# Rotary attention with a channel mix on one core: both parts of a pair's product with V in one stretch

## Chip, cores and metric

The kernel runs on one core of a Trainium2 chip (trn2). The metric is the device time of one execution in microseconds (us), as the median of several runs. Everything below is read from one execution that the hardware profiler recorded.

## What is computed

For 8 batches, 8 heads, 576 positions and a head size of 64, q and k get a rotary embedding, softmax attention is computed, and its output x (8 x 576 x 512) goes through a channel mix with 1024 hidden channels:

```
q_rot, k_rot = rotate(q), rotate(k)
scores = (q_rot @ k_rot.T) / 8
attn = exp(scores - max) / (sum + 1e-9)
x = attn @ v                                  # heads side by side: B, S, 512
xk = mu_k * x + (1 - mu_k) * x_prev           # x_prev: x one position earlier
xr = mu_r * x + (1 - mu_r) * x_prev
out = sigmoid(xr @ w_r) * (relu(xk @ w_k) ** 2 @ w_v)
```

## The kernel before

**Pairs and units.** Two heads make a pair, and there are 32 pairs, 4 to a batch. A pair's 576 query positions are cut into five units (`plan_unit`, L422): units 0 to 3 hold 128 positions of both heads and use the array in two row halves of 64, and unit 4 holds the last 64 positions of both heads in one full-height product. A unit's scores are written by TensorE (L439), reduced to the negated maximum by VectorE (L450), and exponentiated by ScalarE with the row sums as a by-product (L460).

**Plain and split.** Score products come in two kinds. In a plain pair the operands are taken as fp32 (one product per half of the keys, which the trace shows as two instructions). In a split pair q and k are cut into a rounded high part and a remainder, and three products of the faster type fp32r are added up. Splitting takes, for q and for k, one copy (L280 or L282, the high part) and one subtraction (L276, the low part) more than a plain pair needs. `PLAIN` = 5 makes pairs 0 to 4 plain.

**Turning the probabilities.** The product with V needs the keys on the partitions. Pairs 0 to 3 (`EARLY`) are turned by TensorE (L485). From pair 4 on, VectorE transposes blocks of 32 x 32 (L465), one DMA writes the result to DRAM (`turned`, L528) and another reads it back (`rows`, L532). This goes in two parts per pair: part 0 is units 0 and 1 (256 columns for TensorE), part 1 is units 2 to 4 (320 columns). There is one buffer of `rows` for each part, and one buffer for the pair's V (`values`).

**The product with V** (`plan_values`, L542) is, for each part, one item of the plan: 20 matrix products (L557) into one PSUM tile. VectorE then multiplies by the inverse row sums (L564, L569), which have come over DRAM (`sums` to `inv` to `rb`, L507, L513). The channel mix of a batch reads x only after both parts of the pairs concerned (`d["X", half]` holds the results of both).

**The channel mix** (`plan_channel_mix`, L696) makes the mixed operands (L608 to L613), splits them, and runs products of full array height and width, three per step (L637, L638, L639).

**What sets the order.** Nothing is ordered by hand. `Plan.op` takes each item with an engine, a rank, a modelled cost, its predecessors and its buffers. `Plan.issue` (L113 to L210) plays the whole program through a small model: whenever an engine is free, it takes the ready item of least rank, and the order found there is the order in which every engine's instructions, and SP's DMA issues, stand in the program. The ranks come from the constants `R`, `EARLY_R`, `PB`, `MB` and the biases `B_...`. For TensorE an item has a class (0 full array, 1 row halves, 2 the product with V in column halves); a change of class costs `SWITCH` in the model, and `STICK` lightly favours the class at hand. On the chip, the array is used in those three shapes.

Of the kernel before, what the change touches and what calls it, by code (L numbers as in the profile page):

```python
# [23 lines left out]

P = 128
PT = 18
PLAIN = 5
GROUPS = ((0, 1), (2, 3, 4))
WG = (128, 160)
EARLY = 4  # L30
R = dict(k=593.56, q=-116.24, v=661.21, cs=925.67, mu=674.34, ld=2714.96, rope0=616.81, rope1=2781.36, rope2=-26.1,
         split0=3595.69, split1=-1160.76, u0=-579.99, u1=-488.68, u2=-113.46, u3=-1056.0, u4=-253.44, mx=-366.15,
         ex=-1682.84, tp=733.33, di=882.16, dm=-14.89, da=-1213.51, dw=-1363.97, dr2=1693.46, av=2178.52,
         ah=176.61, nr=-1468.99, ev=-1092.53, m0=94.65, mh=99.21, mk=-452.8, mr=761.94, ms=243.4, mx1=50.11,
         mx2=-219.51, mx3=-849.63, mg=17.74, mv=10.72, dr=-638.56, key0=-1530.69, key1=1921.97, key2=337.31,
         gate0=1607.52, gate1=71.52, wk0=458.16, wk1=557.26, wr0=-1023.28, wr1=-291.81, wv0=-546.55, wv1=82.66)
EARLY_R = dict(k=-702.46, q=-1811.61, v=-1186.3, ld=-2648.41, rope0=1279.56, rope1=1357.91, rope2=-489.45,
               split0=-2142.88, split1=2554.98, u0=579.81, u1=-2897.73, u2=-1335.35, u3=-546.57, u4=-1160.48,
               mx=1309.7, ex=308.02, tp=-2491.01, di=1519.96, dm=-694.43, da=-742.07, dw=-1706.94, dr2=1268.99,
               av=-49.56, ah=1124.92, nr=848.06, ev=-2067.99)  # L40
PB = (-3437.67, -442.86, -1619.42, -811.31, 1408.72, -35.97, -277.17, 549.82)
B_COPY, B_ROPE, B_SPLIT, B_LOW, B_MIX, B_SQUARE, B_RELU = -1693.57, -394.58, 857.22, 1457.27, 1935.83, -1161.27, -1219.61
MB = (-201.34, -365.74, -405.66, -1336.49, 1020.79, -1176.32, -311.37, 202.48)
CY = 12
SWITCH, STICK = 195, 20.0
BUFS = dict(nat=2, kh=2, kl=1, qh=2, ql=1, vs=1, pe=4, pe3=8, p0=1, p1=1, s=2, s3=3, nm=6, sums=2, rb=1, pt0=1, pt1=1, t=2, xT=5, raw=2, mxf=2, mxh=5, mxl=5, acc=2, hr=2, kkh=8, kkl=8, rt=3)


# [8 lines left out]
def dve(n):  # L57
    return 1.04 * n + 70
# [16 lines left out]
class Plan:  # L75
# [37 lines left out]
    def issue(self):  # L113
        ops = self.ops
        wait = [len(o[4]) + len(o[6]) for o in ops]
        then = [[] for _ in ops]
        for i, o in enumerate(ops):
            for x in o[4]:
                then[x].append(i)
        left = {s: s.users for f in self.families.values() for s in f}  # L120
        follows = {}
        for f, slots in self.families.items():
            slots.sort(key=lambda s: (s.group, ops[s.opener][1], s.index))
            for n, s in enumerate(slots):
                s.index, s.wait = n, int(n >= self.bufs[f]) + int(n > 0 and slots[n - 1].opener != s.opener)
                if n > 0 and slots[n - 1].opener != s.opener:
                    follows.setdefault(slots[n - 1].opener, []).append(s)
        behind = [[] for _ in ops]
        for i, o in enumerate(ops):
            for x in {s.opener for s in o[5]} - {i}:  # L130
                behind[x].append(i)
                wait[i] += 1
        ready = {e: [] for e in self.LATENCY}
        busy = {e: False for e in self.LATENCY}
        port = {"V": 0.0, "G": 0.0}
        events = []
        now, engine, last = 0.0, {}, 0

        def met(i):
            wait[i] -= 1  # L140
            if wait[i] == 0:
                for e in ops[i][0]:
                    heapq.heappush(ready[e], (now if e == "D" else ops[i][1] + ops[i][0][e][1], i))

        def grant(s, producer=None):
            s.wait -= 1
            if s.wait <= 0:
                if producer is None:
                    met(s.opener)
                else:  # L150
                    later(producer, s.opener)

        def later(producer, o):
            heapq.heappush(events, (now + self.LATENCY[producer][next(iter(ops[o][0]))], 1, o))

        def finish(i, e):
            for x in then[i]:
                later(e, x)
            for s in ops[i][5]:
                left[s] -= 1  # L160
                if left[s] == 0:
                    slots = self.families[s.family]
                    if s.index + self.bufs[s.family] < len(slots):
                        grant(slots[s.index + self.bufs[s.family]], e)

        for i, w in enumerate(wait):
            if w == 0:
                wait[i] = 1
                met(i)
        for slots in self.families.values():  # L170
            for s in slots:
                if s.wait == 0:
                    met(s.opener)
        while True:
            for e, queue in ready.items():
                while queue and not busy[e]:
                    if e == "T":
                        best = min(queue, key=lambda x: (x[0] + STICK * (self.cls[x[1]] != last), x[1]))
                        queue.remove(best)
                        i = best[1]  # L180
                    else:
                        _, i = heapq.heappop(queue)
                    if i in engine:
                        continue
                    engine[i] = e
                    ops[i][3](e)
                    for s in follows.get(i, ()):
                        grant(s)
                    for x in behind[i]:
                        met(x)  # L190
                    busy[e] = True
                    cost, _, shared = ops[i][0][e]
                    if e == "T":
                        cost += SWITCH * (self.cls[i] != last)
                        last = self.cls[i]
                    start = now
                    if shared:
                        start = max(now, port["G" if e == "V" else "V"])
                        port[e] = start + cost
                    heapq.heappush(events, (start + cost, 0, i))  # L200
            if not events:
                break
            now, kind, i = heapq.heappop(events)
            if kind == 1:
                met(i)
                continue
            busy[engine[i]] = False
            finish(i, engine[i])
        assert len(engine) == len(ops), [(i, ops[i][0], ops[i][1], wait[i]) for i in range(len(ops)) if i not in engine][:20]
        return now  # L210
# [3 lines left out]
def rope_attention_channel_mix(ctx, tc, qt, kt, v, cs, mu, w_k, w_v, w_r, out):  # L214
# [4 lines left out]
    B, NP, _, _, S = kt.shape  # L219
# [202 lines left out]
    def plan_unit(t, d, c):  # L422

        heads = (0, 1) if c < 4 else (0,)
        w = {}
# [12 lines left out]
                        r = (up, dn)[x] if c < 4 else whole  # L438
                        T.matmul(w[x][:, h, 0:H], lhsT=kind(d[q][r, c * P:(c + 1) * P]), rhs=kind(d[k][r, h * H:(h + 1) * H]), start=i == 0, stop=i == len(todo) - 1)  # L439

        m = op("T", t, (1100 if d["plain"] else 770) if c < 4 else (1072 if d["plain"] else 804), products, d["q"] + d["k"] + ([] if d["early"] else early_done), slots + d["sq"] + d["sk"], int(c < 4))
        for x in heads:
            u = 4 if c == 4 else c + 5 * x
            g = int(c >= 2)
# [49 lines left out]
    def plan_move(t, d):  # L494
# [18 lines left out]
            nc.sync.dma_start(d["rb"][(up, dn)[x]], src)  # L513

        c4 = op("A", t + d["r"]["ex"] + 0.2, 170, lambda: A.copy(d["sums"][:, 9:10], d["sums"][:, 4:5]), [d["E", 4]], [ss])
        o = op("V", t + d["r"]["nr"], 400, inverse, [c4] + [d["E", u] for u in range(9)], [ss])
        o = dma(t + d["r"]["dw"], P * 128, write, [o], [ss])
        d["R"] = [dma(t + d["r"]["dr2"] + 0.1 * x, D * 4 * 640, lambda x=x: read(x), [o], [sr]) for x in range(2)]
        d["sr"] = sr
# [22 lines left out]
    def plan_values(t, d):  # L542


        w, e = {}, [[], []]
        sx = d["sx"] = Slot("xT")
        for g in range(2):
            s_a = Slot("t")
# [17 lines left out]
            def divided_last(x):  # L566
                r = (up, dn)[x]
                acc = w[1][:, 0:384].rearrange("p (a n) -> p a n", a=4)[r, :, 80 - 80 * x:96 - 80 * x]
                V.tensor_tensor(out=d["x"][r, 513:S + 1].rearrange("p (a n) -> p a n", n=16), in0=acc, in1=d["rb"][r, :, 128 + 16 * x:144 + 16 * x], op=ALU.mult)  # L569

            o = op("T", t + d["r"]["av"] + d["r"]["ah"] * g, 2120 + 490 * g, products, d["M", g] + [d["v"]], [s_a, d["sv"], d["spt", g]], 2)
            e[g] = [op("V", t + d["r"]["ev"] + d["r"]["ah"] * g, dve(256) + 30, divided, [o] + d["R"], [s_a, sx, d["sr"]])]
            if g:
                e[g] += [op("V", t + d["r"]["ev"] + d["r"]["ah"] * g + 0.1 * x, dve(64) + 30, lambda x=x: divided_last(x), [o] + d["R"], [s_a, sx, d["sr"]]) for x in range(2)]
        z = op("G", t + d["r"]["ev"], 110, lambda: G.memset(d["x"][:, 0:1], 0.0), [], [sx])
        d["X", 0], d["X", 1] = e[0] + e[1] + [z], e[0] + e[1]

# [220 lines left out]
```

## Time and profile before

| | |
|---|---|
| median of 3 runs | 974.1 us (970.01 to 974.42) |
| profiled execution | 972.62 us, span in the trace 970.8 us |
| TensorE busy (matrix products) | 905.7 us, 93% |
| VectorE busy | 793.9 us, 82% |
| ScalarE busy | 574.0 us, 59% |
| GpSimd busy | 501.1 us, 52% |
| DMA | 248.23 MB, 256 GB/s on average |
| mean granted TensorE clock | 0.985 of full speed |

TensorE's matrix products overlap in the trace: one is shown with about 0.3 us, and the next starts 0.13 us later. What one costs is read from start to start, not from its length.

### The profile page before, as it was taken

The numbers are of one execution on the slowest core, as the hardware profiler recorded it, in microseconds if no ns is written. First come the engines' busy times: TensorE is split into PE (matmuls) and PEld (weight loads), VectorE is DVE, ScalarE is ACT, GpSimd is POOL, SyncE is SP. The second block draws the span as 40 slices with busy tenths as digits, with TensorE's granted clock in tenths as the row PEclk, the third lists the DMA queues.
The fourth block names the chain that finished last, engine by engine and source line by source line (L and its number), as shares of the span: only waits on it lengthen the run. The fifth ranks groups of instructions, "written<-read, shape, count | busy, mean of one in ns | idle before, by whom it ended". The sixth has DMA issues, their size and how long they took to land.

```text
span 970.8 us, 18627 instructions
## 1 busy us (share of the span) xinstructions
PE 905.7 (93%) x6938; PEld 758.1 (78%) x6938; DVE 793.9 (82%) x1348; ACT 574.0 (59%) x1414; POOL 501.1 (52%) x491
## 2 busy tenths in 40 slices
PE   0767879999899999999999999989999999999998
PEld 0444558888688788888988888777898888888998
DVE  5787898898788988989897879978986988974652
ACT  4776767675566665755665647647665656734243
POOL 6766764563566646666265636356654734601201
PEclk9898999999899999999999999999999999999999
DMA  7553538979999979986978688798976788793000
GB/s 251 159 172 120 163 99 301 381 277 340 338 321 336 331 267 347 332 303 232 324 270 290 198 314 305 260 371 313 374 256 234 275 306 271 255 373 95 20 26 25
DMA packets 98107, 248.23 MB, mean 256 GB/s; under 512 B 11360, under 2 KB 43104, under 8 KB 90848
## 3 DMA queue, kind: packets, MB, share of 16 engines
q1 hardware_dynamic: 98016, 247.04, 72.0%
q8 instruction: 54, 0.88, 0.4%
q14 instruction: 37, 0.30, 0.1%
HBM read 154.47 MB, written 92.54 MB: 254 GB/s over the span
## 4 chain that ended last, share of the span: by engine, by line
PE 73%; DMA 13%; DVE 6%; ACT 3%; POOL 2%; issue 2%; SPq 1%; DVEq 0%; ACTq 0%; POOLq 0%
PE acc L637 17%; PE acc L638 14%; PE acc L639 14%; PE av L557 14%; PE scores L439 12%; DMA rb<-inv 4%; DMA rows<-turned 2%; DMA values<-in_v 2%; DVE nm L450 2%; DMA inv<-sums 2%; PE turn L485 1%; DMA xk<-in_kt 1%; DVE p L465 1%; ACT early L460 1%; DMA turns<-in_cs 1%
## 5 line engine op out<-in xcount | busy, mean ns | idle before, releaser
L460 ACT ACTIVATE pe<-scores,nm 128x576 f32<-128x576 f32 x252 | 184.7, 737 | 127.0 <-DVE nm L450 126.4
L450 DVE TENSOR_REDUCE nm<-scores 128x1 f32<-128x576 f32 x288 | 206.0, 747 | 43.8 <-PE scores L439 42.3
L465 DVE STREAM_TRANSPOSE p<-pe 128x576 f32<-128x576 f32 x252 | 186.1, 760 | 5.9 <-ACT pe L460 5.3
L557 PE MATMUL av<-rows,values 128*64 128x320 f32 (+1 forms) x1280 | 170.6, 414 | 6.3 <-DMA rows<-turned 2.4
L637 PE MATMUL acc<-mxh,wk_h 128*128 128x288 f32 x512 | 158.8, 310 | 3.4 <-DVE mxh L282 2.4
L637 PE MATMUL acc<-kkh,wv_h 128*128 128x288 f32 x512 | 155.4, 303 | 0.7 <-DVE rt L693 0.6
L276 POOL TENSOR_TENSOR mxl<-mxf,mxh 128x288 fp32r<-128x288 f32 x90 | 79.0, 883 | 145.7 <-ACT mxh L280 102.7
L638 PE MATMUL acc<-mxl,wk_h 128*128 128x288 f32 x512 | 151.0, 295 | 1.1 <-POOL mxl L276 1.1
L638 PE MATMUL acc<-kkl,wv_h 128*128 128x288 f32 x512 | 151.1, 295 | 0.0
L639 PE MATMUL acc<-kkh,wv_l 128*128 128x288 f32 x512 | 151.0, 295 | 0.0
L639 PE MATMUL acc<-mxh,wk_l 128*128 128x288 f32 x512 | 150.6, 294 | 0.0
L557 PEld LDWEIGHTS av<-rows,values 128*64 128x64 f32 x1280 | 88.7, 138 | 68.0 <-issue 14.6
L439 PE MATMUL scores<-kh,qh 64*128 64x288 f32 (+1 forms) x666 | 112.5, 390 | 25.5 <-POOL qh L276 20.2
L276 POOL TENSOR_TENSOR kkl<-hr,kkh 128x288 fp32r<-128x288 f32 x95 | 82.0, 873 | 82.5 <-ACT kkh L280 68.5
L276 POOL TENSOR_TENSOR xq<-xq,turns 128x128 f32<-128x128 f32 (+1 forms) x79 | 82.7, 1062 | 62.5 <-DMA xq<-in_qt 62.5
L439 PEld LDWEIGHTS scores<-kh,qh 64*128 64x128 f32 (+1 forms) x666 | 64.3, 197 | 63.8 <-issue 25.2
L637 PEld LDWEIGHTS acc<-mxh,wk_h 128*128 128x128 f32 x512 | 96.4, 188 | 18.5 <-issue 10.1
L637 PEld LDWEIGHTS acc<-kkh,wv_h 128*128 128x128 f32 x512 | 96.2, 188 | 10.6 <-issue 7.5
L638 PEld LDWEIGHTS acc<-mxl,wk_h 128*128 128x128 f32 x512 | 96.6, 189 | 1.6 <-POOL mxl L276 1.5
L639 PEld LDWEIGHTS acc<-mxh,wk_l 128*128 128x128 f32 x512 | 96.4, 188 | 0.0
L638 PEld LDWEIGHTS acc<-kkl,wv_h 128*128 128x128 f32 x512 | 96.3, 188 | 0.0
L639 PEld LDWEIGHTS acc<-kkh,wv_l 128*128 128x128 f32 x512 | 96.2, 188 | 0.0
(86 smaller groups left out, 1822.0 us busy)
## 6 DMA issues: line engine op xcount, KB each, us to landing
rows<-turned SPq DMA_DIRECT2D x28, 1600.0 KB, 9.2
turned<-p SPq DMA_DIRECT2D x28, 1440.0 KB, 9.7
rows<-turned SPq DMA_DIRECT2D x28, 1280.0 KB, 7.1
turned<-p SPq DMA_DIRECT2D x28, 1152.0 KB, 8.0
xq<-in_qt SPq DMA_DIRECT2D x32, 640.0 KB, 5.4
xk<-in_kt SPq DMA_DIRECT2D x32, 576.0 KB, 6.9
values<-in_v SPq DMA_DIRECT2D x32, 320.0 KB, 5.9
rb<-inv SPq DMA_DIRECT2D x64, 160.0 KB, 6.7
```

The lines of the kernel that those rows point to most:

```text
L276: (V if e == "V" else G).tensor_tensor(out=out, in0=a, in1=b, op=op)
L439: T.matmul(w[x][:, h, 0:H], lhsT=kind(d[q][r, c * P:(c + 1) * P]), rhs=kind(d[k][r, h * H:(h + 1) * H]), start=i == 0, stop=i == len(todo) ...
L450: V.tensor_reduce(out=w["nm", x], in_=w[x][:, :, 0:H], op=ALU.max, axis=AX.XY, negate=True)
L460: A.activation(w["p", x].rearrange("p (h n) -> p h n", h=2), w[x][:, :, 0:H], AF.Exp, bias=w["nm", x], scale=1.0, accum_out=d["sums"][:, u ...
L465: V.transpose(d["p", g][:, :, at:at + 32], w["p", x].rearrange("p (b n) -> p b n", n=32))
L485: T.transpose(a[i][0:n, k * P:(k + 1) * P], w["p", x][:, j * P:j * P + n], early["ident"])
L557: T.matmul(acc[(up, dn)[x], :, to:to + n], lhsT=d["vf"][:, 5 * x + j, :], rhs=rows_t[g][:, :, j, n * x:n * x + n], start=j == 0, stop=j == 4)
L637: T.matmul(w["a"], lhsT=w_h[:, i, sl], rhs=x["h"], start=(i == 0), stop=False)
L638: T.matmul(w["a"], lhsT=w_h[:, i, sl], rhs=x["l"], start=False, stop=False)
L639: T.matmul(w["a"], lhsT=w_l[:, i, sl], rhs=x["h"], start=False, stop=(i == count - 1))
```

## The change

Four edits. The two parts of a pair become one item for TensorE, which waits for both parts' probabilities, takes both PSUM tiles, and runs the 40 products one after the other; the VectorE items behind it are the same ones, and wait for the one item. `PLAIN` goes from 5 to 4, so that pair 4 is split. The model's costs change: `SWITCH` becomes three values by the class that is left, and some item costs differ, which has no instruction of its own. And all constants of the ranks are new, so that the order of the whole program is another one.

```diff
-PLAIN = 5
+PLAIN = 4
...
-R = dict(k=593.56, q=-116.24, v=661.21, cs=925.67, mu=674.34, ld=2714.96, rope0=616.81, rope1=2781.36, rope2=-26.1,
+R = dict(k=806.48, q=2.09, v=1204.78, cs=333.97, mu=282.75, ld=3341.61, rope0=832.31, rope1=2583.52, rope2=-136.93,
...
-PB = (-3437.67, -442.86, -1619.42, -811.31, 1408.72, -35.97, -277.17, 549.82)
+PB = (-4531.28, -645.33, -1851.98, -1094.7, 1367.95, -32.7, -655.54, 484.84)
...
-SWITCH, STICK = 195, 20.0
+SWITCH, STICK = (93, 220, 189), 20.0
...
-                        cost += SWITCH * (self.cls[i] != last)
+                        cost += SWITCH[last] * (self.cls[i] != last)
...
-        m = op("T", t, (1100 if d["plain"] else 770) if c < 4 else (1072 if d["plain"] else 804), products, d["q"] + d["k"] + ([] if d["early"] else early_done), slots + d["sq"] + d["sk"], int(c < 4))
+        m = op("T", t, (1080 if d["plain"] else 770) if c < 4 else (756 if d["plain"] else 804), products, d["q"] + d["k"] + ([] if d["early"] else early_done), slots + d["sq"] + d["sk"], int(c < 4))
...
-        o = op("V", t + d["r"]["nr"], 400, inverse, [c4] + [d["E", u] for u in range(9)], [ss])
+        o = op("V", t + d["r"]["nr"], 585, inverse, [c4] + [d["E", u] for u in range(9)], [ss])
...
-        w, e = {}, [[], []]
+        w, e, parts = {}, [[], []], []
...
-            o = op("T", t + d["r"]["av"] + d["r"]["ah"] * g, 2120 + 490 * g, products, d["M", g] + [d["v"]], [s_a, d["sv"], d["spt", g]], 2)
-            e[g] = [op("V", t + d["r"]["ev"] + d["r"]["ah"] * g, dve(256) + 30, divided, [o] + d["R"], [s_a, sx, d["sr"]])]
-            if g:
-                e[g] += [op("V", t + d["r"]["ev"] + d["r"]["ah"] * g + 0.1 * x, dve(64) + 30, lambda x=x: divided_last(x), [o] + d["R"], [s_a, sx, d["sr"]]) for x in range(2)]
+            parts.append((products, divided, s_a))
+
+        def both():
+            for f, _, _ in parts:
+                f()
+
+        o = op("T", t + d["r"]["av"], 4730, both, d["M", 0] + d["M", 1] + [d["v"]], [x[2] for x in parts] + [d["sv"], d["spt", 0], d["spt", 1]], 2)
+        for g, (_, f, s_a) in enumerate(parts):
+            e[g] = [op("V", t + d["r"]["ev"] + d["r"]["ah"] * g, dve(256), f, [o] + d["R"], [s_a, sx, d["sr"]])]
+        e[1] += [op("V", t + d["r"]["ev"] + d["r"]["ah"] + 0.1 * x, dve(64) + 85, lambda x=x: divided_last(x), [o] + d["R"], [s_a, sx, d["sr"]]) for x in range(2)]
```

## Rows read from the trace of the kernel before

**Rows 1.** Windows of core 0: us, then busy us of each engine, granted clock, DMA, GB/s.

```profile
0.00:150.00 150.00, 100.75 (x611) 65.88 (x612) 117.83 (x183) 101.65 (x227) 102.97 (x91) 0.93 0.51 165
100.00:125.00 25.00, 21.66 (x143) 14.15 (x141) 20.60 (x36) 19.45 (x43) 19.20 (x16) 0.95 0.51 157
150.00:900.00 750.00, 737.39 (x5822) 624.91 (x5821) 640.94 (x1090) 450.13 (x1136) 388.06 (x389) 1.00 0.83 296
900.00:971.00 71.00, 67.57 (x511) 67.33 (x509) 35.12 (x76) 22.21 (x53) 10.05 (x12) 0.99 0.06 22
```

**Rows 2.** The page, part 4: the chain that ended last, by engine.

```profile
PE 73%; DMA 13%; DVE 6%; ACT 3%; POOL 2%; issue 2%; SPq 1%; DVEq 0%; ACTq 0%; POOLq 0%
```

**Rows 3.** TensorE in time: stretches ahead of channel mix, first and last of 27.

```profile
206.96 0.29 PE L639 MATMUL acc<-mxh,wk_l 128*128 128x288 f32 x1
207.18 2.91 PE L557 MATMUL av<-rows,values 128*64 128x320 f32 x20
210.03 0.40 PE L637 MATMUL acc<-mxh,wk_h 128*128 128x288 f32 x1
210.26 0.29 PE L638 MATMUL acc<-mxl,wk_h 128*128 128x288 f32 x1
210.39 0.29 PE L639 MATMUL acc<-mxh,wk_l 128*128 128x288 f32 x1
...
886.34 2.91 PE L557 MATMUL av<-rows,values 128*64 128x320 f32 x20
889.19 0.40 PE L637 MATMUL acc<-kkh,wv_h 128*128 128x288 f32 x1
```

**Rows 4.** The same view: stretches ahead of scores, first and last of 29.

```profile
159.61 2.38 PE L557 MATMUL av<-rows,values 128*64 128x256 f32 x20
161.92 0.54 PE L439 MATMUL scores<-kh,qh 64*128 64x288 f32 x4
...
162.91 0.40 PE L637 MATMUL acc<-mxh,wr_h 128*128 128x288 f32 x1
...
858.15 2.38 PE L557 MATMUL av<-rows,values 128*64 128x256 f32 x20
860.46 0.53 PE L439 MATMUL scores<-kh,qh 64*128 64x288 f32 x4
```

**Rows 5.** The same view: an early pair in one stretch, last of 4.

```profile
129.06 5.07 PE L557 MATMUL av<-rows,values 128*64 128x256 f32 x40
134.06 1.24 PE L439 MATMUL scores<-kh,qh 64*128 64x288 f32 x8
```

**Rows 6.** The same view: a plain unit (pair 4), then a split one.

```profile
139.43 1.24 PE L439 MATMUL scores<-kh,qh 64*128 64x288 f32 x8
140.60 0.40 PE L637 MATMUL acc<-mxh,wk_h 128*128 128x288 f32 x1
...
148.10 0.54 PE L439 MATMUL scores<-kh,qh 64*128 64x288 f32 x4
...
149.09 0.40 PE L637 MATMUL acc<-mxh,wk_h 128*128 128x288 f32 x1
```

**Rows 7.** Groups by form, 60 to 200 us: making and splitting q and k.

```profile
L280 ACT CAST qh<-xq 128x640 fp32r<-128x640 f32 x3 | 2.2, 731 | 1.1 <-DVE xq L276 1.1
L280 ACT CAST kh<-xk 128x576 fp32r<-128x576 f32 x3 | 2.0, 673 | 0.0
L276 POOL TENSOR_TENSOR ql<-xq,qh 128x640 fp32r<-128x640 f32 x1 | 2.0, 1987 | 0.0
L276 DVE TENSOR_TENSOR kl<-xk,kh 128x576 fp32r<-128x576 f32 x1 | 0.9, 915 | 0.0
```

**Rows 8.** Waits of TensorE: us in total, times, longest us.

```profile
PE av L557 <- DMA rows<-turned: 2.4, 2, 1.6
```

**Rows 9.** The page, part 6: loads of probabilities, KB, us to landing.

```profile
rows<-turned SPq DMA_DIRECT2D x28, 1600.0 KB, 9.2
rows<-turned SPq DMA_DIRECT2D x28, 1280.0 KB, 7.1
```

## What the change does to the time: the prediction

> **What bounds the kernel now.** I read the windows first. From 150 to 900 us TensorE is busy for 737.4 of 750 us, at full granted clock; VectorE, next, for 640.9 [rows 1]. The reader is to see a run in three parts: a first stretch of 150 us with 100.7 us of TensorE work (loading, weight conversion, the early pairs), a long stretch that TensorE fills, and a tail of 71 us that it nearly fills. The chain of waits says the same: 73% of the span is TensorE's, 13% DMA [rows 2]. So in the long stretch a microsecond less on TensorE is a microsecond less on the clock, as long as nothing else runs late, and 12.6 us of idle time is all that other engines and transfers cost there. In the first 150 us the other engines count.
>
> Then I read TensorE in order of time, from start to start. A channel-mix product follows the one before it by 0.13 us (from 210.26 to 210.39). A stretch of the product with V starts 0.22 us after the last channel-mix product, 0.09 more; it takes 2.85 us for part 1, and the second channel-mix product behind it comes 0.23 us after the first, 0.10 more [rows 3]. Part 0 takes 2.31 us [rows 4].
>
> **The change, part by part.**
>
> *One stretch in place of two.* The early pairs already have both parts side by side: 40 products from 129.06 to 134.06, 5.00 us, where apart they take 2.31 + 2.85 = 5.16 [rows 3 to 5]. I take 0.15 us saved inside a stretch. Of the 56 stretches of the 28 later pairs, none stands beside its partner now, so 28 x 0.15 = 4.2 us go. This is the firm part of the sum.
>
> *Changes of array shape.* Each pair also loses one visit, but what its two ends cost depends on what stands behind it. Behind 27 of the 56 comes a channel-mix product, and both ends are paid: 0.09 + 0.10 = 0.19 us [rows 3]. Behind 29 come scores; there the scores take 0.99 us up to the next channel-mix product [rows 4], as they do behind a channel-mix product [rows 6], and their own entry is saved, so that taking the stretch away saves nothing more at the ends. With the same mix, 28 x 27/56 = 13.5 visits lose 0.19 us each: 2.6 us. The ends are 0 (all removed ones stood ahead of scores) and 28 x 0.19 = 5.3 us.
>
> *Pair 4 split.* On TensorE a plain unit takes 1.17 us and a split one 0.99 [rows 6]: 4 x 0.18 = 0.7 us less. The fifth unit has another shape and is left at 0 (between 0 and another 0.18). For this the copies and subtractions of q and k are added, ahead of its first scores (a later unit of it stands at 139.43 [rows 6]). The nearest rows are those of the next pair: 0.73 + 0.67 us on ScalarE, 1.99 on GpSimd, 0.92 on VectorE [rows 7]. In the window from 100 to 125 us ScalarE has 5.5 us free, GpSimd 5.8, VectorE 4.4, and TensorE itself 3.3 [rows 1]. Their cover is this free time; without it all four lie on the path, 4.3 us. The other end is 0. I take VectorE's 0.9 us, since it has least to spare.
>
> Against this may stand a contention. A subtraction took 1.99 us on GpSimd and 0.92 on VectorE, and whether either engine stood in the other's way these rows don't tell [rows 7]. The Trainium skill (GPSIMD Engine Reference, Key points) says that GpSimd shares its SBUF interfaces with VectorE, in contention with VectorE's instructions that have two SBUF inputs. By that rule the two added subtractions exclude other work on both engines, and 0.92 + 1.99 = 2.9 us would be added where I take 0.9; the sum would be 2.0 us smaller. No row here shows it, and it stays inside the range.
>
> *The wait.* The one item waits for the later part's probabilities. Loads take 7.1 us for part 0 and 9.2 for part 1 [rows 9]. Queued behind the waiting item on TensorE is the rest of the program's order; who waits for it is VectorE's division, then the channel mix, which needs both parts now as before, so no reader of x was served by the earlier part alone. Part 0's buffer is held until the shared stretch ends, and with it SP's next load of part 0, with all SP issues queued behind that. A pair has 750/28 = 26.8 us on TensorE, while the round of load and shared stretch takes about 9.2 + 5.0 = 14.2 us: 12 us of cover, so I cost it at 0. Without that cover each part-0 load is late by up to its 7.1 us. What is late next is under the rivals.
>
> *VectorE, the other engines, DMA.* The same divisions, transposes and transfers are issued, in the same number. The model's new costs add no instruction. Both PSUM tiles are taken at once, by an item that follows the previous pair's division by many microseconds: 0.
>
> *The new order.* It moves every instruction on every queue, SP's and GpSimd's too, and no row shows it. Its bounds are the idle time that an order can remove or add: 12.6 us between 150 and 900 [rows 1], so from 12.6 less to as much again more. Nothing in the rows speaks for a sign; I take 0, and half of it (6.3 us) each way for the range.
>
> *Sum:* 4.2 + 2.6 + 0.7 - 0.9 = 6.6 us less. The profiled execution took 972.6 us, so 966.0 in its terms. It lies 1.5 us under the median of the runs, 974.1; with the same offset the median becomes 967.5 us.
>
> **The rivals.**
>
> *TensorE runs dry in front of the shared stretch (slower).* Place: the pairs whose part 1 lands just when it is needed. There part 0's 2.31 us used to fill the wait and now comes behind it. For it: TensorE waited twice on these loads, 2.4 us together, once 1.61 us, with nothing else to run [rows 8]. Against it: only 2 of 56. Price: 2.31 us per such pair. Three pairs eat the gain (6.6/2.31), five make the kernel slower by over 0.5%. Where it decides I take every fourth pair, 7 x 2.31 = 16.2 us: 983.7 us.
>
> *The saved time comes back as idle time (no change).* If VectorE (85% busy in the long stretch) or the transfers (0.83 of the DMA engines) set the pace, TensorE ends each stretch earlier and waits [rows 1]. For it: both are high. Against it: TensorE idles for only 1.7% of that stretch, so it, and not they, is at its limit. All 6.6 us lost: 974.1 us. An order in which the parts stood together anyway would do the same; the rows exclude it, as 56 stretches of 20 stand apart.
>
> *The new order also removes what idle time there is (faster).* Between half of the 12.6 us and all of it, 9.4 us taken: 958.1 us. For it: the waits are scattered and short, of a kind that an order can mend. Against it: this order had the same freedom.
>
> **How the numbers follow.** About 0.5%, 4.9 us, is what a measurement of this kernel can tell from no change. Forecast 0.55, its own range 960 to 975 (the order's 6.3 us and the ends of the other terms); running dry 0.13; given back 0.20; idle time removed 0.12. Faster by over 0.5% means under 969.2: 0.43 of the forecast's 0.55, all of the last rival, and 0.03 of the second, 0.58. Slower means over 979.0: 0.10 of the first rival's 0.13 and 0.01 of the second, 0.11. The rest, 0.31, is no change. The range reaches from under the last rival to the bound of slower, 956 to 979; outside it are the 0.11 and about a third of the last rival, 0.04.
>
> **What would show it right or wrong.** In the changed profile the product with V should show as 32 stretches of 40 products with 5.00 us from start to start, and TensorE's busy time should fall by about 7 us from 905.7. In the long stretch its idle time should stay near 12 us. Pair 4's units should take 0.99 us. The sum is wrong if waits on loads of probabilities grow past 7 us (the first rival), if busy time falls and the span does not (the second), or if the span falls by much more than busy time (the third). If the first 150 us become longer by over 3 us, the splitting of pair 4 was not covered.

## The result, and the profile after

The changed kernel takes 957.32 us (median of 4, 953.74 to 959.5) against 972.06 before (median of 4, one run more than in the table): a ratio of 0.9848, 95% interval 0.9815 to 0.9881, or 14.7 us less. The forecast was 967.5 us. Its direction was right, and the result lies inside the wide range of 956 to 979; but it lies outside the forecast's own range of 960 to 975, and the sum of its terms was 6.6 us, less than half of what came.

The same windows of the changed kernel, with the last one up to its end (span 957.5 us; columns as in [rows 1]):

```profile
0.00:150.00 150.00, 104.89 (x616) 68.18 (x617) 118.24 (x178) 100.13 (x226) 99.77 (x88) 0.92 0.52 171
150.00:900.00 750.00, 744.17 (x5938) 640.45 (x5937) 651.57 (x1093) 452.36 (x1144) 412.14 (x413) 1.00 0.82 295
900.00:958.00 58.00, 53.87 (x407) 53.64 (x406) 27.56 (x59) 20.96 (x50) 8.39 (x10) 1.00 0.06 21
```

With [rows 1] this splits the 13.3 us by which the span fell. After 150 us TensorE was busy for 737.39 + 67.57 = 804.96 us of 820.8 and is now for 744.17 + 53.87 = 798.04 of 807.5. So 6.9 us are less busy time, and 6.4 us are less idle time (15.8 to 9.5).

Less busy time is not the same as less work, for two reasons. First, the kernel before has a stretch at half the clock in it, which set in during its longest stop, the one at 252 us (see the last section):

```profile
256.30:263.10 6.80, 5.53 (x24) 3.51 (x25) 4.58 (x8) 3.29 (x9) 1.55 (x2) 0.50 1.07 371
```

At the full clock the 5.53 us of products there would have taken about half (an estimate), so some 2.8 us of the 6.9 are the lower clock; the changed kernel has no such stretch between 150 us and its last product. Second, the two kernels had come to different places at 150 us. These are their channel-mix products (tile `acc`) up to there, before and after:

```profile
0.00:150.00 150.00, 12.59 (x79) 10.83 (x80) 1.64 (x4) 0.82 (x2) 0.93 0.51 165
```
```profile
0.00:150.00 150.00, 10.63 (x54) 9.06 (x55) 0.46 (x1) 1.11 (x3) 0.92 0.52 171
```

The changed kernel has 25 products more left to do, at 0.13 us each, and one unit of scores less (222 score products are done by 150 us, for 192, but 1434 are left for 1446), at 0.99: 2.3 us more work. What the products themselves save is thus about 6.9 - 2.8 + 2.3 = 6.4 us. In all, **6.4 us are saved on the products, 6.4 us are idle time that is gone, 2.8 us are lower clock that is gone, and 2.3 us are taken back by a first stretch that got less far**. That last part seems to belong to this execution: in runs e4 and e5 below, which have the same order up to 150 us, 76 and 72 such products were done by then.

In the chain that ended last, DMA fell from 13% to 5% [rows 2]:

```profile
PE 78%; DVE 7%; DMA 5%; ACT 4%; issue 3%; POOL 2%; SPq 0%; DVEq 0%; POOLq 0%; ACTq 0%
```

TensorE in order of time (columns as in [rows 3]): first a unit of pair 4's scores, then a shared stretch ahead of channel mix, then one ahead of scores, and the one shared stretch with a wait in it.

```profile
116.69 0.53 PE L439 MATMUL scores<-kh,qh 64*128 64x288 f32 x4
...
117.69 0.55 PE L485 MATMUL turn<-early 128*128 128x128 f32 x3
...
190.86 0.29 PE L645 MATMUL acc<-kkh,wv_l 128*128 128x288 f32 x1
191.09 5.07 PE L557 MATMUL av<-rows,values 128*64 128x256 f32 x40
196.09 0.40 PE L643 MATMUL acc<-kkh,wv_h 128*128 128x288 f32 x1
196.33 0.29 PE L644 MATMUL acc<-kkl,wv_h 128*128 128x288 f32 x1
...
217.29 5.07 PE L557 MATMUL av<-rows,values 128*64 128x256 f32 x40
222.30 0.53 PE L439 MATMUL scores<-kh,qh 64*128 64x288 f32 x4
...
223.29 0.40 PE L643 MATMUL acc<-mxh,wr_h 128*128 128x288 f32 x1
...
440.28 2.38 PE L557 MATMUL av<-rows,values 128*64 128x256 f32 x20
443.33 2.91 PE L557 MATMUL av<-rows,values 128*64 128x320 f32 x20 [0.67 <-DMA rows<-turned]
```

A shared stretch takes 5.00 and 5.01 us from start to start in the first two places; its entry takes 0.23 us and its exit 0.24, about as the single ones did [rows 3]. The Trainium skill (TensorEngine Tiling (Array Packing), Key Properties) says that a change of tiling mode drains TensorE. The trace fits this in so far as some 0.1 us more sits at either change; that it is a drain, no run here shows. The 28 pairs now have fewer such changes. A split unit of pair 4 takes 1.00 us for the plain 1.17 [rows 6]. Of the 28, 10 stand ahead of channel mix. Two waits of TensorE (us in total, times, longest):

```profile
PE scores L439 <- ACT pe L460: 2.4, 2, 1.9
PE av L557 <- DMA rows<-turned: 0.7, 1, 0.7
```

The wait for probabilities, 2.4 us before [rows 8], did not grow. The one that is left (0.67 us) stands inside a shared stretch, ahead of part 1: on the chip part 0's products did not wait for part 1. The model alone treats the 40 products as one item.

### The profile page after: what moved, and what is told of

The parts are those of the page before. It is cut to its first block, busy times and chain, and to the rows that moved or that the text cites. A ratio compares the mean times of both kernels' runs of the same rounds, so it can differ in the third digit from the quotient of the medians.

```text
span 957.5 us, 18658 instructions
## 1 busy us (share of the span) xinstructions
PE 902.9 (94%) x6956; PEld 762.3 (80%) x6956; DVE 797.4 (83%) x1328; ACT 573.5 (60%) x1419; POOL 520.3 (54%) x510
## 4 chain that ended last, share of the span: by engine, by line
PE 78%; DVE 7%; DMA 5%; ACT 4%; issue 3%; POOL 2%; SPq 0%; DVEq 0%; POOLq 0%; ACTq 0%
PE acc L643 18%; PE acc L644 16%; PE acc L645 16%; PE scores L439 14%; PE av L557 13%; DVE nm L450 2%; PE turn L485 1%; DMA rows<-turned 1%; DVE p L465 1%; DMA turned<-p 1%; DMA turns<-in_cs 1%; DMA xq<-in_qt 1%; ACT early L460 1%; DMA xk<-in_kt 1%; ACT pe L460 1%
## 5 line engine op out<-in xcount | busy, mean ns | idle before, releaser
L276 POOL TENSOR_TENSOR mxl<-mxf,mxh 128x288 fp32r<-128x288 f32 x98 | 83.3, 853 | 170.7 <-ACT mxh L280 126.7
L557 PE MATMUL av<-rows,values 128*64 128x320 f32 (+1 forms) x1280 | 163.8, 411 | 1.6 <-ACT rows L280 0.9
L276 POOL TENSOR_TENSOR xq<-xq,turns 128x512 f32<-128x512 f32 (+1 forms) x81 | 93.1, 1163 | 46.0 <-DMA xq<-in_qt 38.9
```

The source lines that it names most:

```text
L276: (V if e == "V" else G).tensor_tensor(out=out, in0=a, in1=b, op=op)
L557: T.matmul(acc[(up, dn)[x], :, to:to + n], lhsT=d["vf"][:, 5 * x + j, :], rhs=rows_t[g][:, :, j, n * x:n * x + n], start=j == 0, stop=j == 4)
```

## The experiments

An experiment on an order meets a difficulty here: each edit makes the model play the program anew, and then everything moves. So there are two kinds of runs. *Played anew* means that the model finds its own order from the edited program. *Order held* means that the order is first found for the unedited program and then written out with the edit alone in it. Ratios are to the kernel before, run on the same chip; the changed kernel's is 0.9848.

**One edit each, played anew.** The shared stretch put into the kernel before, the two items put back into the changed one, and pair 4 plain in the changed one:

In e1 `plan_values` is the changed kernel's, in e2 that of before, and in e3 one constant differs:

```diff
-            o = op("T", t + d["r"]["av"] + d["r"]["ah"] * g, 2120 + 490 * g, products, d["M", g] + [d["v"]], [s_a, d["sv"], d["spt", g]], 2)
...
+        o = op("T", t + d["r"]["av"], 4730, both, d["M", 0] + d["M", 1] + [d["v"]], [x[2] for x in parts] + [d["sv"], d["spt", 0], d["spt", 1]], 2)
...
-PLAIN = 4
+PLAIN = 5
```

> The kernel before with the shared stretch alone: old ranks, old model costs, PLAIN = 5; the model plays out another order from the same ranks. Theory A (the shared stretch is worth some 7 us by itself and the rest of the 14.7 us is the new order's fewer stalls): 965 us, 7 less than before, 32 stretches of 40, and idle time of TensorE between 150 and 900 us near the 12.6 us of before. Theory B (the shared stretch also removes the stalls, and the ranks matter little): 957 to 960 us, with idle time falling to about half. Theory C (old ranks do not fit the shared item, TensorE runs dry ahead of it): 972 us or more, with waits of the product with V on its loads above 7 us.

> The changed kernel with the two parts as two items again (new ranks, new SWITCH, PLAIN = 4 kept), order played out anew. Theory A: 957.3 + 7 = 964 us, with TensorE's idle time between 150 and 900 us as low as in the changed kernel, about 6 us. Theory B: 970 us or more, with the idle time back at 12 us or above.

> The changed kernel with PLAIN = 5, so that pair 4 is plain again, order played out anew. If splitting pair 4 is worth what TensorE saves on it less what cannot be hidden, it makes no difference that can be measured: 957 us, within 3. Rival (splitting pair 4 carries some of the unforecast gain): over 961 us. Rival (its copies and subtractions were not covered): under 954 us.

Measured: 1001.59 us (ratio 1.0326, 1.0305 to 1.0347), 995.52 (1.0260, 1.0221 to 1.0298), 1014.13 (1.0455, 1.0418 to 1.0493). All three are 25 to 44 us slower than the kernel before, even with pair 4 alone changed. The theories that named a time missed it. Three that were open upwards were met in the time: e1's theory C, though its waits for loads were 1.5 us and not above 7; e2's theory B, with its idle time (21.5 us between 150 and 900 us); and e3's first rival. But such a size is too much for the edits, and raised the question what a new play costs by itself.

**The same program, another play.** One modelled cost is moved by a few units; no instruction is added or removed, but the order changes, and some instructions go to another engine where the model has the choice.

In e7 (changed kernel), e13 (changed kernel) and e12 (kernel before), in that order, each line shown up to its cost and what follows it:

```diff
-        o = op("T", t + d["r"]["av"], 4730, both,
+        o = op("T", t + d["r"]["av"], 4740, both,
...
-        o = op("T", t + d["r"]["av"], 4730, both,
+        o = op("T", t + d["r"]["av"], 4720, both,
...
-            o = op("T", t + d["r"]["av"] + d["r"]["ah"] * g, 2120 + 490 * g, products,
+            o = op("T", t + d["r"]["av"] + d["r"]["ah"] * g, 2125 + 490 * g, products,
```

> The changed kernel with the modelled cost of the shared stretch at 4740 instead of 4730: the same instructions and ranks, but the model's play goes another way, and many places of the order with it. Theory G (the ranks fit one play of the model and no other, so that the three kernels with an order played anew were slow for that and not for what they changed): 2 to 6% slower than the changed kernel, 975 to 1015 us, with more idle time spread over the long stretch. Theory H (they were slow for what they changed): 957 us within 3.

> The changed kernel with the modelled cost of the shared item at 4720 instead of 4730, a second draw of the nudge that cost 1.0 to 1.2% before. Theory G: again slower than the changed kernel by 0.5 to 4%. If the first nudge was only unlucky: 957 us within 3.

> The kernel before with the modelled cost of its part-0 item at 2125 instead of 2120: same instructions and ranks, another play. Theory G (ranks fit one play only, in the kernel before as in the changed one): 0.5 to 4% slower than before, 976 to 1010 us. Theory K (only the changed kernel's ranks are that finely fitted): within 0.5% of before.

Measured: e7 966.79 us (ratio 0.9962, 0.9944 to 0.9979), e13 1016.31 (1.0479, 1.0431 to 1.0527), e12 1016.83 (1.0498, 1.0463 to 1.0533). This is theory G for both kernels, though all three sizes lie outside the ranges given: against the 0.9848 of the changed kernel the two nudges cost 1.1 and 6.3 points (2 to 6% and 0.5 to 4% were expected), and the kernel before loses 5.0 (0.5 to 4%). The long stretch of e7, e13 and e12, in that order:

```profile
150.00:900.00 750.00, 737.12 (x5858) 631.28 (x5858) 645.44 (x1094) 441.92 (x1119) 403.55 (x407) 1.00 0.81 294
```
```profile
150.00:900.00 750.00, 710.14 (x5526) 605.18 (x5525) 626.82 (x1058) 432.60 (x1098) 394.45 (x398) 0.97 0.81 290
```
```profile
150.00:900.00 750.00, 706.93 (x5462) 593.92 (x5462) 639.34 (x1055) 419.73 (x1065) 381.91 (x382) 0.97 0.81 289
```

TensorE is idle for 12.9, 39.9 and 43.1 us there. What a nudge changes is how often engines wait for one another, and in e13 and e12 the granted clock too (0.97). The ranks fit one play, and the other plays were 1 to 6% slower, where the whole change is worth 1.5. So e1 to e3 say nothing on their edits.

**The shared stretch pulled apart, order held.** In e4 part 1 comes one TensorE item later, in e5 part 0 one item earlier. On the other four engines' queues not one instruction changes place.

The core of e4, where `held` is written out behind the next item of TensorE, and of e5, where `seq` is the order found for the changed kernel:

```diff
+        def second():
+            parts[1][0]()
+
         def both():
-            for f, _, _ in parts:
-                f()
+            parts[0][0]()
+            if d["early"]:
+                second()
+            else:
+                held.append(second)
...
+                    late = self.held[:] if e == "T" else []
                     ops[i][3](e)
+                    for f in late:
+                        f()
+                        self.held.remove(f)
...
+    def ahead(seq):
+        out = list(seq)
+        for o, first in shared.items():
+            at = [n for n, (i, e) in enumerate(out) if not callable(i) and (i == o or e == "T")]
+            here = next(n for n in at if out[n][0] == o)
+            out.insert(at[at.index(here) - 1], (first, "T"))
+        return out
```

> The changed kernel with its order held on every engine and queue; only TensorE's part 1 of the 28 later pairs is moved behind the next item of TensorE, which is channel mix in 10 cases and scores in 18. Theory A (a stretch pays at both of its ends): 28 x 0.15 + 10 x 0.19 = 6.1 us more, 963.4 us, and no new stalls. Theory D (these ends are hidden, and the gain is all from the order): 957 us, within 2.

> The changed kernel with its order held on every engine and queue; only TensorE's part 0 of the 28 later pairs is put one item earlier, ahead of the item in front of the shared stretch (channel mix in 26 cases, scores in 2), so that no result comes later than by the cost of the visit itself. Theory A (visits cost what the rows say, and the rest of what pulling part 1 back cost was its lateness): 28 x 0.15 + 26 x 0.19 = 9.1 us more than the changed kernel, about 966.5 us. Theory E (apart costs more than visits, wherever the odd part stands): 970 us or more, as with part 1 behind. Theory D (visits are hidden): 957 to 959 us.

Measured: e4 970.2 us (ratio 1.0003, 0.9982 to 1.0024), e5 971.25 (0.9994, 0.9973 to 1.0015). Both give back all of the gain, some 15 and 14 us by their ratios, where 6.1 and 9.1 were expected. TensorE after 150 us in e4 (span 968.6 us), then in e5 (969.4):

```profile
150.00:900.00 750.00, 739.13 (x5817) 624.55 (x5816) 641.16 (x1071) 448.63 (x1133) 403.32 (x407) 1.00 0.81 293
900.00:1010.00 110.00, 65.28 (x493) 65.05 (x492) 34.28 (x74) 21.78 (x52) 10.11 (x12) 0.99 0.04 14
```

```profile
150.00:900.00 750.00, 741.04 (x5822) 626.27 (x5819) 641.76 (x1072) 449.04 (x1135) 403.44 (x407) 1.00 0.82 293
900.00:1010.00 110.00, 65.63 (x496) 65.39 (x494) 34.30 (x74) 21.79 (x52) 10.13 (x12) 0.99 0.04 14
```

Busy time is 739.13 + 65.28 = 804.41 us in e4 and 806.67 in e5, 6.4 and 8.6 more than in the changed kernel. As above, this is not yet the price of the visits. Channel-mix products up to 150 us, and the time at the lower clock, in e4 and then in e5:

```profile
0.00:150.00 150.00, 13.85 (x76) 12.05 (x77) 0.46 (x1) 1.92 (x5) 0.93 0.54 179
790.90:794.30 3.40, 3.40 (x18) 1.64 (x15) 2.97 (x3) 0.72 (x1) 3.32 (x3) 0.50 0.28 102
```
```profile
0.00:150.00 150.00, 13.28 (x72) 11.49 (x72) 0.46 (x1) 1.92 (x5) 0.93 0.53 177
477.70:481.10 3.40, 3.40 (x16) 3.40 (x16) 2.65 (x6) 1.55 (x4) 1.28 (x1) 0.50 0.93 273
```

The changed kernel had done 54 such products by 150 us, and one unit of scores less than e4 and e5. So e4 and e5 have 3.9 and 3.3 us less to do after 150 us, and 1.7 us of their busy time are the lower clock. **The visits cost 8.6 us in e4 and 10.2 in e5, where the rows said 6.1 and 9.1**: they are real, and somewhat dearer than forecast. On top comes idle time, 14.2 and 12.7 us where the changed kernel has 9.5, and the 1.7 us of lower clock. The three together are 15.0 and 15.2 us, close to the 15 and 14 us by the ratios.

Scores waiting for exponentials come to this in e4 and in e5, for 2.4 us in the changed kernel:

```profile
PE scores L445 <- ACT pe L466: 6.3, 7, 2.1
```
```profile
PE scores L449 <- ACT pe L470: 5.3, 6, 1.9
```

So a third of a microsecond per pair that the order was not made for also brings new waits. VectorE's waits for the product with V grow from 14.7 us to 28.0 in e4, but only to 16.7 in e5, so that how a visit becomes a wait is not shown for e5. Theory A is right that visits cost, and wrong that nothing else follows; that it is not a matter of which part is moved (theory E) e5 shows.

**The shared stretch in the old order, order held.** In the kernel before, the earlier part of each later pair is moved next to the other, with its division and the clearing of x's first column behind it, and, in 8 cases, the next load into its buffer too.

```diff
+            one, two = sorted((0, 1), key=lambda g: at[d["av", g]])
+            first, last = d["av", one], d["av", two]
+            div = [x for x in d["div"][one]] + [d["z"]]
+            move = [x for x in div if at[x] < at[last]]
...
+            out[n:n + 1] = [entries[first], out[n]] + [entries[x] for x in sorted(move, key=lambda x: at[x])] + [entries[x] for x in loads]
```

> The kernel before with its order held; only part 0 (or whichever part came first) of the 28 later pairs is moved next to the other part, with its division, the clearing of the first column and, in 8 cases, the next load into its buffer moved behind. PLAIN = 5 and old ranks. 11 of the removed stretches stood ahead of channel mix. Theory A: 28 x 0.15 + 11 x 0.19 = 6.3 us less than before, ratio about 0.9935, with the stalls of before. Theory F (the later loads and divisions make new waits that eat it): ratio 0.998 or above. Theory B (the shared stretch alone gives most of the result): 0.988 or below.

Measured: 1010.89 us, ratio 1.0417 (1.0380 to 1.0454): theory F, at six times the size of the gain that it was to eat. TensorE after 150 us (span 1006.7 us), then its scores' waits for the exponentials and VectorE's waits for the product with V:

```profile
150.00:900.00 750.00, 715.48 (x5576) 608.09 (x5576) 617.36 (x1047) 435.99 (x1105) 382.25 (x381) 0.98 0.81 288
900.00:1010.00 110.00, 101.19 (x749) 95.60 (x745) 52.79 (x118) 34.64 (x81) 14.28 (x18) 0.99 0.19 65
```

```profile
PE scores L449 <- ACT pe L470: 22.5, 29, 3.1
```

```profile
DVE xT L595 <- PE av L588: 39.3, 27, 3.0
```

and the same two waits in the kernel before:

```profile
PE scores L439 <- ACT pe L460: 4.8, 8, 1.8
```

```profile
DVE xT L564 <- PE av L557: 8.1, 11, 3.1
```

ScalarE's waits for the maxima, before and in e8, and TensorE's wait for loads in e8:

```profile
ACT pe L460 <- DVE nm L450: 126.4, 92, 6.2
```
```profile
ACT pe L470 <- DVE nm L460: 158.0, 95, 8.2
PE av L588 <- DMA rows<-turned: 2.4, 3, 1.1
```

Idle time after 150 us is 40.0 us for 15.8, and busy time 816.7 for 805.0, with the granted clock at 0.98 in the long stretch. The later loads of probabilities are not what TensorE waits for: 2.4 us, as before [rows 8]. VectorE's instructions run in the order of its queue. Moved behind the shared stretch, the division holds VectorE in 27 places for 39.3 us; ScalarE then waits 31.6 us more for the maxima, which VectorE makes, and 29 times TensorE stands before scores whose tiles are not free. That the maxima are late for the division ahead of them is read from the queue; no run moved the divisions alone. In the slow nudge e13 the same two waits read 21.5 us (19 times) and 37.0 us (26 times). In the changed kernel VectorE's wait is this:

```profile
DVE xT L564 <- PE av L557: 14.7, 14, 2.3
```

So the order of the kernel before, with these moves alone, cannot use the shared stretch. In the new one VectorE meets it too early 14 times and not 27.

**Pair 4 plain, order held.** The two copies and two subtractions are not there, the sums stand at the copies' places, and the scores are plain.

```diff
+        as_plain = d["bg"] == PAIRS[4]
...
+        def high(e):
+            if as_plain:
+                combine(m["e"], f32(part(n + "h")), m["c"], m["s"], ALU.add)
+            else:
+                copy(e, part(n + "h"), m["c"])
```

> The changed kernel with its order held, but pair 4 plain again: its two copies and two subtractions are left out, the sums of q and k stand where the copies were planned, and its scores are plain. Forecast by the rows: TensorE 0.7 us more, up to 0.9 us of VectorE off the path: no difference that can be measured, 957 us within 2. Rival (pair 4's split carries some of the unforecast gain): 961 us or more.

Measured: 957.36 us, ratio 0.9860 (0.9827 to 0.9893), as expected: splitting pair 4 makes no difference that can be measured. Played anew (e3) pair 4 plain had come out 6.1 points slower than the changed kernel.

**A second buffer for V, order held.** Before, the longest stop of the long stretch lies at 252 us. TensorE there, with what ended each idle time:

```profile
254.26 0.40 PE L439 MATMUL scores<-kh,qh 64*128 64x288 f32 x1 [1.76 <-ACT pe L460]
254.98 0.52 PE L439 MATMUL scores<-kh,qh 64*128 64x288 f32 x3 [0.32 <-ACT pe L460]
...
257.57 0.70 PE L557 MATMUL av<-rows,values 128*64 128x256 f32 x2 [1.54 <-DMA values<-in_v]
```

In e10 (kernel before) and e11 (changed kernel) alike, with `spare` a buffer of the weights' conversion:

```diff
-            d["vf"] = values_t[sv.index % BUFS["vs"]]
+            d["vf"] = values_t[0]
+            if n >= 8 and n % 2:
+                if "t" not in spare:
+                    spare["t"] = sb.tile([P, 512, 2], U32, tag="raw", name="raw", bufs=BUFS["raw"])
+                d["vf"] = spare["t"].rearrange("p n w -> p (n w)")[:, 0:10 * D].bitcast(F32).rearrange("p (a n) -> p a n", a=10)
```

> The kernel before with its order held, and a second buffer for V: from pair 8 on every second pair's V goes into a buffer that the weights' conversion no longer needs, so that SP doesn't wait for the previous pair's last product (67.7 us of SP's waiting before). Theory I (the longest stop of the long stretch, 252 to 261 us with TensorE at half clock behind it, hangs on that load): 2 to 6 us less than before, ratio 0.994 to 0.998, and no such dip of the granted clock between 250 and 262 us. Theory J (the scores' wait on the exponentials holds that place, and the load only came last): no difference, ratio 0.998 to 1.002.

> The changed kernel with its order held and the same second buffer for V, where SP waits 95.8 us in all for the shared stretch to let go of V. If loads queued behind that wait are among what TensorE still waits for: up to 5 us less than the changed kernel, ratio to before 0.980 to 0.984. If they land in time anyway: the changed kernel's 0.985.

Measured: e10 969.85 us (ratio 1.0007, 0.9986 to 1.0029), e11 955.32 (0.9852, 0.9828 to 0.9876). No difference in either: theory J for e10, and the second case of e11. SP's waits for the product with V fell from 67.7 to 30.9 us in e10, and the time stayed. In the place itself another wait ends the stop, at nearly the same length:

```profile
253.25 0.39 PE L445 MATMUL scores<-kh,qh 64*128 64x288 f32 x1 [1.76 <-ACT pe L466]
253.97 0.53 PE L445 MATMUL scores<-kh,qh 64*128 64x288 f32 x3 [0.33 <-ACT pe L466]
...
256.39 4.53 PE L563 MATMUL av<-rows,values 128*64 128x256 f32 x20 [1.36 <-DVE nm L456]
```

The load came last in the profile, but the maxima were next. The same 12.5 us in the kernel before, in e10 and in the changed kernel:

```profile
250.00:262.50 12.50, 8.87 (x58) 5.30 (x55) 9.69 (x17) 6.94 (x16) 5.18 (x5) 0.75 1.05 383
```
```profile
250.00:262.50 12.50, 9.05 (x55) 5.93 (x52) 8.74 (x16) 7.13 (x17) 4.00 (x5) 0.73 1.05 387
```
```profile
250.00:262.50 12.50, 12.50 (x105) 11.51 (x104) 12.39 (x21) 8.50 (x23) 8.80 (x9) 1.00 0.94 353
```

In the first two TensorE is busy for 8.9 and 9.1 us at 0.75 and 0.73 of the clock; in the new order there is no stop here. No run here was faster than the changed kernel beyond the intervals.

## Why the prediction was right, and where its size was off

- *What bounds the kernel:* right. TensorE's saved work came off the span, and no other engine took over. But 12.6 us of idle time was not all that the stops cost: the clock in [rows 1], 1.00, is rounded, and 2.8 us of the busy time were lower clock behind one stop.
- *One stretch in place of two, 4.2 us; changes of array shape, 2.6 us; pair 4's scores, 0.7 us:* right in mechanism and about right in size. The first two, 6.8 us, fall after 150 us, where the products saved about 6.4; pair 4's scores lie before. Stretches take 5.00 us. Ends saved: 27 stretches stood ahead of channel mix, now 10, so 17 x 0.19 = 3.2 us in place of 2.6. Pulled apart in the held order, visits cost 8.6 and 10.2 us where the rows gave 6.1 and 9.1.
- *Total busy time should fall by about 7 us:* it fell by 2.8 only (905.7 to 902.9), since the stretch up to 150 us has 4.1 us more of it, though less channel mix was done there. Where TensorE often waits, and the clock moves, its busy time does not measure its work. A span that falls by much more than busy time was the prediction's own sign of the third rival, and it came: 13.3 us against 2.8.
- *Pair 4's copies and subtractions, 0.9 us on the path:* too small to see; e9 gives a difference of 0.12 points in ratios whose intervals are about 0.33 wide to each side. For the same reason no run separates it from the 2.9 us by the rule of the Trainium skill (GPSIMD Engine Reference, Key points) on shared SBUF interfaces.
- *The wait, 0:* right for the loads; the wait for probabilities even fell. The first rival did not come. It had part 0's products wait for part 1's load; the one time that load was late (443 us), TensorE ran part 0 first and then waited 0.67 us for part 1. But the forecast named VectorE's division as the one that waits and stopped there: it did not ask what is queued behind the division on VectorE. In e8 this is what most likely cost 40 us.
- *The new order, taken as 0 with 6.3 us to each side:* **this is the step that was off.** Idle time after 150 us fell by 6.4 us, of it 6.8 between 150 and 900 us, and with the stop at 252 us went 2.8 us of lower clock, which the bounds did not hold. That is 9.2 us, the amount of the third rival (9.4), which had a chance of 0.12; its 958.1 us came within 0.8 us of the result. That the result lies inside the range at all is owed to the range reaching down to that rival.
- *The reason for taking 0,* that nothing speaks for a sign, was not right either. The bounds of 12.6 us to each side belonged to orders that are fitted. e7, e12 and e13 show that an order that is not fitted to its program loses 1 to 6%. In the one try with the old ranks (e1) the shared stretch was 3.3% slower, so as far as that try shows a gain needed new ranks that fit. How well they fit could not be read from the rows of the kernel before.

What stays open: how much of these 9.2 us a fitted order for two separate items could also have had. Ranks and orders did not carry over from one structure to the other (e1, e2, e8), so no run here separates a better order from a structure that allows one. It was not tried to fit ranks anew.

## What to carry to other kernels

Where a model plays out a program's order from tuned ranks, an edit is tested only with the order held; played anew, even 2125 for 2120 in one modelled cost made this kernel 5% slower. When an item is merged or moved, follow what is queued behind its consumer on the consumer's own engine: in e8 that queue is the likely place where a merge worth 6 us turned into a loss of 40. When busy time is compared, look whether the same work stands in the two windows, and at which clock. And a wait that "came last" is worth removing only if the next one is much earlier: two V buffers took away half of a queue's waiting and no time at all.

## What the runs showed of the hardware

The stop at 252 us cost more than its idle time. TensorE, at full granted clock until then, was busy for 0.42 of 2.5 us, and this and the next windows of the kernel before read:

```profile
252.50:255.00 2.50, 0.42 (x3) 0.20 (x3) 2.43 (x5) 1.62 (x5) 1.21 (x1) 1.00 1.04 409
255.00:257.50 2.50, 1.03 (x11) 0.79 (x11) 2.47 (x6) 2.08 (x6) 0.75 (x2) 0.77 1.03 399
257.50:260.00 2.50, 2.43 (x12) 1.65 (x14) 2.50 (x4) 2.39 (x6) 0.79 (x2) 0.50 1.05 369
260.00:262.50 2.50, 2.50 (x12) 1.26 (x9) 0.91 (x3) 0.12 (x1) 0.00 (x0) 0.50 1.12 343
```

With 0.77 and then 0.50 of the clock granted, a stretch of part 0, which takes 2.31 us elsewhere [rows 4], took 4.5 us behind this stop, at the lower level of 1.2 GHz. So a part of such a stop's price, 2.8 us here, stands under busy time, and doesn't show as a wait. The lower clock in e4 and e5 also stands within 2 us behind the longest stop of the long stretch (2.1 us at 790 us, 1.9 us at 476 us). But length alone does not decide it: e10 has a stop of 2.07 us at 665 us, and the clock behind it stayed at 1.00.
